# Moving LayerNorm steps, two stores and a vector sum around the down products of a fused attention and feed-forward kernel

## The chip, the cores and the metric

The kernel runs on one core of a Trainium2 chip. The metric is the time of one execution on the device in microseconds (us). Times given as start times count from the start of the profiled span. The engines are TensorE (PE in the profile, its weight load PEld), VectorE (DVE), ScalarE (ACT), GpSimd (POOL) and SyncE (SP). SyncE does no arithmetic here: it issues nearly all DMAs, in the order in which the program gives them.

## The reference

The input x has 2048 rows of 640 columns. It is normalised row by row; the normalised rows go into an attention with 32 heads of 192 columns over the last 512 keys of a cache, and into a gated feed-forward of width 1536. The two results are multiplied and added to x.

```python
x = A_x
xn = _layernorm(x, axis=-1)                  # (x - m) / sqrt(v + 1e-5)
q = (xn @ wq).reshape(B, Sq, 32, 192)        # 32 heads
k, v = the last W = 512 rows of k_cache, v_cache
p = softmax(q k^T * 192 ** -0.5)
s = (p v, heads side by side) @ wo
g = silu((silu(xn @ w_gate) * (xn @ w_up)) @ w_down)
return x + s * g
```

All inputs and the output are bfloat16.

## The kernel before

The kernel first does the feed-forward for all 2048 rows and leaves g in DRAM (`g_d`); then come the attention and the output product. The order of the work is written out by hand: each engine runs its instructions in the order in which the program emits them, and an engine that has to wait holds up all that is queued behind it on the same engine.

**Blocks and tiles.** The rows are cut into four blocks of 512 rows, numbered 0 to 3, and each block into four tiles of 128 rows, tile t = 4 * block + ti. `normalise(b, ti)` does two things to a tile: `ln_apply` subtracts the mean and scales the rows, in place in `rows_x` (on ScalarE for block 2, L411; on VectorE for blocks 1 and 3, L421), and `ln_transpose_dma` has SyncE issue a DMA transpose that puts the tile into `xnT` (L427), where columns are on partitions. The statistics of block 3 are gathered on ScalarE by eight small steps (`ln_sums`, L391 for sums, L395 for squares); they stand in the list `act_work`, and each call of `act_step()` emits the next of them.

**Halves and pairs.** Blocks 0 and 1 are half 0, blocks 2 and 3 half 1. The hidden layer of a half is computed in 2 x 2 form over the two blocks and over pairs of weight column groups, with seven products W1 to W7 in place of eight (a Strassen-Winograd scheme). `paired(half, g, n)` returns the steps `w1` to `w7` of one pair, each with ten matmuls (L695), and the copies, gates and sums between them. The products need sums of the two blocks: `swap_block` copies a block with its upper and lower partition halves exchanged (two DMAs, L646), which gives `x2s` and `x3s` of a half; `x_sum(half, n, part)` makes X1 to X4 from them on VectorE in two parts each (L655, shown in the profile at the line L490 of the helper `total`). For half 1, X1 is block 3 minus block 2, X2 is x3s minus X1, X3 is x3s minus block 3, and X4 is x2s minus X2. W2 of a pair uses x2s, W5 uses X1, W6 X2, W7 X3, W3 x3s. X1 of half 1 is written over the `rows_x` rows of block 3, so it needs these rows transposed first, as it needs `xnT` of both blocks.

**Downs.** `ffn_down(b, u)` does the down product of two tiles of block b, u = 0 or 1, again as seven products W1 to W7, each of six matmuls (L518). Its steps are numbered n = 0 to 6, in the order w1, w2, w6, w5, w7, w3, w4. ScalarE copies partial results and applies the outer SiLU (`gate`, L524) into the two tiles `g[0]` and `g[1]`, out of a pool of four `g_t` buffers. The last two gates of a down are kept back in the list `trailing`, and then two stores in the list `stores`; `finish_down` emits both, or with `False` the gates alone. A store (L527) is a DMA to `g_d`.

**The order around the change.** `run_pairs(0, ...)` ends with the last pair of half 0. Then the four downs of half 0 run in the order (b, u) = (1, 0), (1, 1), (0, 0), (0, 1), numbered m = 0 to 3; between their steps the loop of L1016 places the remaining statistics, the normalisation of blocks 2 and 3, the swaps x2s and x3s of half 1, and `load_pairs(0)`, eight DMAs with the weights of the second column group (L318 and L319). After the loop come `x_sum(1, 0, ...)`, further loads, and the pairs of half 1. After the pairs of half 1, `q_full` computes the first six q tiles in full (five matmuls each, L748, and a copy on ScalarE, L752), the first two directly one after the other and the others among the downs of half 1. PSUM tiles of two banks come from `sc_tile()` (two buffers, `sc`) and `mm_tile()` (`mm`).

Of the kernel before, what the change touches and what calls it, by code (L numbers as in the profile page):

```python
# [15 lines left out]
def kernel(  # L16
# [13 lines left out]
    nc = tc.nc  # L30
# [47 lines left out]
    def sc_tile():  # L78
        return sc_pool.tile([P, 2, 512], f32, name="sc")
# [172 lines left out]
    def q_of(i, j):  # L252
        pr, b = divmod(i, NB)
        half, k = divmod(b, 2)
        return q_pair(phase_of(pr, half))[:, 2 * k + j, :] if j < 2 else q_joint(half)[:, 2 * k + pr % 2, :]
# [4 lines left out]
    with ExitStack() as fctx:  # L260
# [243 lines left out]
        def ffn_down(b, u, then=None):  # L504
# [19 lines left out]
                nc.scalar.activation(g[side][:, n * HC : (n + 1) * HC], x, ACT.Silu)  # L524

            def store(side):
                nc.sync.dma_start(out=g_d[4 * b + u + 2 * side, :, :], in_=g[side][:])  # L527

            early_half = b == 2 and u == 0

# [72 lines left out]
        def finish_down(send=True):  # L603
            while trailing:
                trailing.pop(0)()
            while send and stores:
                stores.pop(0)()
# [133 lines left out]

            return dict(w1=w1, keep=keep, w2=w2, w5=w5, w6=w6, w7=w7, w3=w3, w4=w4, gate_2=gate_2, gate_3=gate_3, gated=gated)

        def q_full(i, j):
            pr, b = divmod(i, NB)
            q_ps = sc_tile()[:, 0, :]
            for c in range(NC):
                nc.tensor.matmul(  # L748
                    q_ps[:, :], w_all[:, weights_of(pr, j)[0], weights_of(pr, j)[1], c, :], xnT[:, c, b * 512 : (b + 1) * 512],
                    start=(c == 0), stop=(c == NC - 1),  # L750
                )
            nc.scalar.copy(q_of(i, j), q_ps[:, :])  # L752

        def swap_x(to, half, b):

# [189 lines left out]
        def run_pairs(half, steps, work, extra, k0=0):  # L945

            b0 = (1, 2)[half]
            earlier = steps[k0 - 1] if k0 else None
            for k in range(k0, len(steps)):
                final = k == len(steps) - 1  # L950
                now = steps[k]
                if k == 2:
                    earlier["w7"]()
                now["w1"]()
                if k == 1:
                    earlier["w3"]()
                now["keep"]()
                act_step()
                if earlier:
                    if k != 2:  # L960
                        earlier["w7"]()
                    if not final:
                        earlier["gate_3"]()
                now["w2"]()
                for do in work.get(k, ()):
                    do()
                if final:
                    if half == 0:
                        left_sum(b0, 0, 2)
                        wd_sum(2)  # L970
                    now["w6"]()
                    earlier["gate_3"]()
                    now["w5"]()
                    earlier["w4"]()
                    earlier["gate_2"]()
                    earlier["gated"](3)
                    now["w7"]()
                    if half:
                        earlier["gated"](2)
                    now["gate_3"]()  # L980
                    now["w3"]()
                    now["gated"](3)
                    downs = ffn_down(b0, 0, (b0, 1))
                    downs.pop(0)()
                    now["w4"]()
                    if half == 0:
                        ahead_1.append(ffn_down(1, 1, (0, 0)))
                    now["gate_2"]()
                    if half == 0:
                        nc.scalar.copy(p1_1, owns[1][:, 1, 0:HC])  # L990
                        act_step()
                        for n in range(2):
                            left_sum(b0, 0, n)
                        gated_late.extend(step["gated"] for step in (earlier, now))
                    if half:
                        now["gated"](2)
                        for n in range(2):
                            left_sum(b0, 0, n)
                    return downs
                now["w5"]()  # L1000
                if earlier:
                    earlier["w4"]()
                    earlier["gate_2"]()
                    for which in (3, 2):
                        earlier["gated"](which)
                now["w6"]()
                if k:
                    now["w3"]()
                earlier = now
                if k in extra:  # L1010
                    extra[k]()
# [4 lines left out]
        for m, (b, u) in enumerate(order):  # L1016
            if m:
                downs = ahead_1[0] if m == 1 else ffn_down(b, u, order[m + 1] if m < 3 else None)
            for n, do in enumerate(downs, 7 - len(downs)):
                do()  # L1020
                if n == 0:
                    finish_down(m != 2)
                if (m, n) in ((0, 3), (1, 0)):
                    act_step()
                if (m, n) in ((1, 6), (2, 3)):
                    for ti in range(2 * m - 2, 2 * m):
                        normalise(3, ti)
                    if m == 2:
                        finish_down()
                        swap_block(x2s, 2)  # L1030
                if (m, n) in ((1, 3), (1, 5)):
                    normalise(2, (n + 1) // 2)
                if m == 2 and n == 4:
                    swap_block(x3s, 3)
                    load_pairs(0)
                if m == 0 and n == 2:
                    wd_sum(3)
                if m == 1 and n == 3:
                    for gated in gated_late:
                        gated(2)  # L1040
        finish_down()
        mm_next[0] = 0
        for b in (2, 3):
            hTs[b] = ffh.tile([P, NF, 512], bf, name="hT")
        for part in range(2):
            x_sum(1, 0, part)
        load_k(0)
        for half in range(2):
            swap_x(DIFF[0], half, half)
# [43 lines left out]
        beside_x(ROWS[1], DIAG)  # L1093
        xwork += sum_x(0) + sum_x(1) + combined_x(ROWS[0], DIFF[1]) + combined_x(ROWS[1], DIAG)
        order = [(b, u) for b in (2, 3) for u in range(2)]
        for _ in range(2):
            q_full(*early_q.pop(0))
        for m, (b, u) in enumerate(order):
            if m:
                downs = ffn_down(b, u, order[m + 1] if m < 3 else None)  # L1100
            for n, do in enumerate(downs, 7 - len(downs)):
                do()
                if n == 0:
                    finish_down()
                if (m, n) == (3, 6):
                    finish_down()
                if (m, n) == (0, 1) or n == 6 and m:
                    q_full(*early_q.pop(0))
                if (m, n) == (2, 4):
                    copy_wq(1, (2,), nc.scalar.copy)  # L1110
                if (m, n) == (0, 4):
                    copy_wq(0, (2,), nc.scalar.copy)
                    load_wq(1)
                for _ in range(((5,), (2, 4, 6), (2, 4, 6), (3,))[m].count(n)):
                    xwork.pop(0)()
# [758 lines left out]
```

## Time and profile before

| | us |
|---|---|
| median of 3 runs | 856.94 |
| range of the runs | 856.87 to 856.99 |
| the profiled execution, whole | 856.42 |
| the profiled execution, span from first to last instruction | 854.6 |
| PE busy | 847.7 |
| VectorE busy | 640.9 |
| ScalarE busy | 472.2 |

The page of the profile gives the busy time of each engine, the DMA queues and the chain of work that ended last. The waits name who waited for whom, and the timeline gives instructions in order of start, neighbours of one kind merged: start, duration, engine, line, operation, output and inputs, count, and in brackets the idle time ahead of it and what ended it. Consecutive matmuls overlap, so that their durations do not add up; the distance between starts is what one costs. SPq and ACTq are the DMA issues in the queues of SyncE and ScalarE.

### The profile page before, as it was taken

How to read it: one execution, taken by the hardware profiler on the slowest of the kernel's cores; microseconds unless marked ns; L12 is line 12 of the kernel's file. 1: busy time of each engine (PE TensorE's matmuls, PEld its weight loads, DVE VectorE, ACT ScalarE, POOL GpSimd, SP SyncE). 2: the span in 40 equal slices, each digit the busy share in tenths (PEclk: the TensorE clock that was granted, in tenths of full speed). 3: DMA queues.
4: the chain of work that ended last, by engine and by line, in shares of the span. 5: the costliest groups of instructions: out<-in, count | busy, mean ns of one | idle time of the engine just before them, and what ended most of it. 6: DMA issues, size and time to landing. Idle time of an engine off the chain costs nothing.

```text
span 854.6 us, 24104 instructions
## 1 busy us (share of the span) xinstructions
PE 847.7 (99%) x10180; PEld 582.7 (68%) x10185; DVE 640.9 (75%) x1113; ACT 472.2 (55%) x638; POOL 173.2 (20%) x259
## 2 busy tenths in 40 slices
PE   9999999999999999999999999999999999999998
PEld 5656556576667667666667667667667777877877
DVE  6797997777758757767767757757757698978787
ACT  5785675657666676676676667667676500001010
POOL 1100000103423323323423323333322000000001
PEclk9999999999999999999999999999999999999999
DMA  9916927646797799998999998899687998191820
GB/s 238 256 16 142 218 76 170 133 94 159 174 172 139 195 180 183 196 208 187 203 192 198 196 173 150 165 213 200 158 178 164 292 273 325 23 329 55 311 82 28
DMA packets 272236, 150.51 MB, mean 176 GB/s; under 512 B 174208, under 2 KB 268032, under 8 KB 272128
## 3 DMA queue, kind: packets, MB, share of 16 engines
q1 hardware_dynamic: 271344, 148.33, 77.6%
q8 instruction: 80, 1.31, 0.6%
q10 hardware_dynamic: 784, 0.65, 0.3%
q14 instruction: 28, 0.23, 0.1%
HBM read 78.54 MB, written 30.41 MB: 127 GB/s over the span
## 4 chain that ended last, share of the span: by engine, by line
PE 97%; DMA 2%; DVE 0%; ACT 0%; issue 0%; SPq 0%; DVEq 0%; ACTq 0%
PE sc L1213 20%; PE acc L1367 16%; PE mm L1251 13%; PE mm L1156 13%; PE sc L1156 7%; PE sc L1251 6%; PE mm L695 4%; PE acc L1563 4%; PE sc L695 3%; PE mm L518 3%; PE sc L436 2%; PE sc L518 2%; PE mm L1144 1%; PE sc L748 1%; DMA xc<-xnT 1%; DMA fa<-in_B_w_gate_dram 1%
## 5 line engine op out<-in xcount | busy, mean ns | idle before, releaser
L1217 ACT ACTIVATE p_t<-sc 128x1024 bf16<-128x1024 f32 x256 | 256.9, 1025 | 93.7 <-PE sc L1213 93.0
L1213 PE MATMUL sc<-q_all,khat 64*128 64x512 bf16 x1536 | 204.2, 376 | 0.0
L1251 PEld LDWEIGHTS <-p_t 64*128 64x128 bf16 x4096 | 179.9, 94 | 35.7 <-POOL turn_t L1229 0.7
L1251 PE MATMUL mm<-V_p,p_t 64*128 64x193 bf16 x2784 | 146.7, 243 | 0.0
L1156 PEld LDWEIGHTS <-w_all 64*128 64x128 f16 (+1 forms) x1540 | 86.7, 94 | 73.3
L1156 PE MATMUL mm<-xc,w_all 64*128 64x512 f16 x950 | 119.3, 376 | 0.0
L1213 PEld LDWEIGHTS <-khat 64*128 64x128 bf16 x1536 | 82.6, 94 | 51.2 <-issue 2.2
L1198 POOL TENSOR_TENSOR m_f<-m_f 128x1024 f32<-128x1024 f32 x44 | 104.8, 2382 | 41.4 <-DVE q_all L1194 40.1
L1194 DVE TENSOR_TENSOR q_all<-mm,m_f 128x1024 bf16<-128x1024 f32 x44 | 53.8, 1223 | 68.9 <-ACT m_f L1191 68.9
L1367 PEld LDWEIGHTS <-a_q 128*128 128x128 bf16 (+1 forms) x888 | 84.0, 98 | 29.5
L1367 PE MATMUL acc<-b_w,a_q 128*128 128x320 bf16 (+2 forms) x720 | 95.7, 295 | 0.0
L1229 POOL MEMSET turn_t<- 128x1 f32 x128 | 12.8, 100 | 317.6 <-PE mm L1251 225.1
L1273 DVE TENSOR_TENSOR O_b<-mm,r 128x384 bf16<-128x384 f32 x142 | 73.8, 553 | 3.2 <-DVE r L1269 0.2
L1204 DVE TENSOR_TENSOR q_all<-mm,m_f 128x1024 bf16<-128x1024 f32 x44 | 53.8, 1222 | 22.9 <-POOL m_f L1198 22.5
L1251 PE MATMUL sc<-V_p,p_t 64*128 64x193 bf16 x1312 | 68.0, 243 | 0.0
L1191 ACT COPY m_f<-sc 128x1024 f32<-128x1024 f32 x37 | 37.5, 1012 | 29.1 <-PE sc L1156 28.9
L1156 PE MATMUL sc<-xnT,w_all 64*128 64x512 bf16 x370 | 46.5, 376 | 0.0
L1507 DVE TENSOR_TENSOR a_q<-a_q 128x3072 f16<-128x3072 bf16 (+1 forms) x24 | 41.8, 1754 | 5.7 <-PE acc L1367 4.2
L695 PEld LDWEIGHTS <-f_more 64*128 64x128 f16 (+1 forms) x480 | 26.3, 94 | 27.4 <-issue 3.9
L1269 DVE RECIPROCAL r<-mm 128x4 f32<-128x4 f32 x87 | 15.7, 180 | 35.5 <-PE mm L1251 33.7
L173 DVE TENSOR_TENSOR w_all<-wq_rows 64x640 f16<-64x640 bf16 x90 | 38.7, 482 | 1.0 <-DMA wq_rows<-in_A_wq_dram 0.5
L1388 POOL TENSOR_TENSOR xc<-xc,xg 128x320 f32<-128x320 f32 x2 | 1.8, 916 | 172.4 <-DVE xc L1404 172.4
(213 smaller groups left out, 1079.7 us busy)
## 6 DMA issues: line engine op xcount, KB each, us to landing
o_d<-OT_b SPq DMA_DIRECT2D x64, 384.0 KB, 3.8
a_q<-o_d SPq DMA_DIRECT2D x32, 768.0 KB, 6.1
wq_rows<-in_A_wq_dram SPq DMA_DIRECT2D x16, 480.0 KB, 5.6
b_w<-in_A_wo_dram SPq DMA_DIRECT2D x16, 480.0 KB, 6.2
wq_rows<-in_A_wq_dram SPq DMA_DIRECT2D x30, 240.0 KB, 6.5
K_p<-in_A_k_cache_dram SPq DMA_DIRECT2D x32, 192.0 KB, 3.5
V_p<-in_A_v_cache_dram SPq DMA_DIRECT2D x32, 192.0 KB, 4.1
xc<-xnT SPq DMA_DIRECT2D x14, 320.0 KB, 5.7
```

The lines of the kernel that those rows point to most:

```text
L518: nc.tensor.matmul(ps, left[:, c, :], D_OF[m][:, c, :], start=(first and c == 0), stop=(c == KD - 1), skip_group_check=True,)
L695: nc.tensor.matmul(ps[:, h, :], left[m][r, c, n * P : (n + 1) * P], right[m][r, c, :], start=(first and c == 0), stop=(c == NC - 1), skip_ ...
L1156: nc.tensor.matmul(ps[:, h, :], ws[h][r, c, :], xs[h][r, c, :], start=(first and c == 0), stop=(c == NC - 1), skip_group_check=True,)
L1194: nc.vector.tensor_tensor(to[:, 1:3, :], st["ps"][:, :, :], m_f[:, 5:3:-1, :], ALU.add)
L1198: nc.gpsimd.tensor_tensor(SIDE, diag, SIDE, ALU.subtract)
L1204: nc.vector.tensor_tensor(to[:, 0:4:3, :], st["ps"][:, :, :], SIDE, ALU.add)
L1213: nc.tensor.matmul(sc[:, h, :], khat[r, j, ks], q_of(i, j)[r, :], start=(j == 0), stop=(j == 2))
L1217: nc.scalar.activation(p_t[:, :, :], sc[:, :, :], ACT.Exp, scale=scale)
L1251: m = nc.tensor.matmul(acc[:, k, h * 256 : h * 256 + Dh + 1], Ps[i][kc][r, h, qt * P : (qt + 1) * P], V_of[i // NB % 2][r, kc, h, 0 : Dh + 1],
L1273: nc.vector.tensor_tensor(O_b[:, k, :, :], a_k[:, :, 0:Dh], r[:, k, :, :].to_broadcast([P, 2, Dh]), ALU.mult,)
L1367: nc.tensor.matmul(ps[:, 0:w], at[:, c, :], b_w[m][:, c, k * w : (k + 1) * w], start=(first and c == 0), stop=(c == KH - 1), skip_group_ch ...
L1507: nc.vector.tensor_tensor(a_s[n, m], x, y, op)
```

## The change

- The two stores of down (1, 1) are issued by ScalarE and no longer by SyncE, and they stand ahead of the last two normalisations of block 3 in the program.
- One `act_step` is emitted in the last pair of `run_pairs`, behind `gate_2` of the pair before, and no longer at step 3 of down m = 0.
- Tiles 2 and 3 of block 2 are normalised at step 3 of downs m = 0 and m = 1, and no longer at steps 3 and 5 of m = 1.
- The swap x3s of half 1 is emitted directly behind x2s, and `load_pairs(0)` at step 0 of m = 3, behind the stores of down (0, 0); before, both stood at step 4 of m = 2.
- The two parts of X1 of half 1 are computed at steps 3 and 5 of m = 3, and no longer after the loop.
- The first two q tiles share one PSUM tile, one in each of its banks: ten matmuls, then two copies.

```diff
             def store(side):
-                nc.sync.dma_start(out=g_d[4 * b + u + 2 * side, :, :], in_=g[side][:])
+                (nc.scalar if (b, u) == (1, 1) else nc.sync).dma_start(out=g_d[4 * b + u + 2 * side, :, :], in_=g[side][:])
...
-        def q_full(i, j):
+        def q_full(*units):
+            ps = sc_tile()
+            for n, unit in enumerate(units):
+                q_matmuls(*unit, ps[:, n, :])
+            for n, unit in enumerate(units):
+                nc.scalar.copy(q_of(*unit), ps[:, n, :])
+
+        def q_matmuls(i, j, q_ps):
             pr, b = divmod(i, NB)
-            q_ps = sc_tile()[:, 0, :]
             for c in range(NC):
...
-            nc.scalar.copy(q_of(i, j), q_ps[:, :])
...
                     earlier["gate_2"]()
+                    act_step()
                     earlier["gated"](3)
...
                 if n == 0:
                     finish_down(m != 2)
-                if (m, n) in ((0, 3), (1, 0)):
+                    if m == 3:
+                        load_pairs(0)
+                if m == 2 and n == 3:
+                    finish_down()
+                if (m, n) == (1, 0):
                     act_step()
                 if (m, n) in ((1, 6), (2, 3)):
                     for ti in range(2 * m - 2, 2 * m):
                         normalise(3, ti)
                     if m == 2:
-                        finish_down()
                         swap_block(x2s, 2)
-                if (m, n) in ((1, 3), (1, 5)):
-                    normalise(2, (n + 1) // 2)
-                if m == 2 and n == 4:
-                    swap_block(x3s, 3)
-                    load_pairs(0)
+                        swap_block(x3s, 3)
+                if n == 3 and m < 2:
+                    normalise(2, 2 + m)
+                if m == 3 and n in (3, 5):
+                    x_sum(1, 0, (n - 3) // 2)
...
-        for part in range(2):
-            x_sum(1, 0, part)
...
-        for _ in range(2):
-            q_full(*early_q.pop(0))
+        q_full(*(early_q.pop(0) for _ in range(2)))
...
-                    q_full(*early_q.pop(0))
+                    q_full(early_q.pop(0))
```

## The prediction

> **What bounds the kernel now.** I read the page first, for the engine that sets the end.
>
> ```profile
> span 854.6 us, 24104 instructions
> PE 847.7 (99%) x10180; PEld 582.7 (68%) x10185; DVE 640.9 (75%) x1113; ACT 472.2 (55%) x638; POOL 173.2 (20%) x259
> PE 97%; DMA 2%; DVE 0%; ACT 0%; issue 0%; SPq 0%; DVEq 0%; ACTq 0%
> ```
>
> TensorE (PE) carries 97% of the chain that ended last. An edit that adds no matmul and removes none can move the time only by the small holes in PE's row. Second view: the waits of PE over the whole span. Besides two waits while the kernel starts up, and one for instruction issue of which I speak below, it has these three.
>
> ```profile
> PE sc L695 <- DMA xc<-xnT: 0.4, 1, 0.4
> PE sc L518 <- ACT q_all L571: 0.3, 1, 0.3
> PE sc L695 <- DVE hT L490: 0.3, 1, 0.3
> ```
>
> Matmul ends are modelled, so the true size of a hole is read from starts. Third view: PE's timeline where the downs of half 0 end and the pairs of half 1 begin.
>
> ```profile
> 78.33 0.98 PE L518 MATMUL mm<-wd_sb,khat 128*128 128x320 f16 x6
> 79.62 0.97 PE L518 MATMUL sc<-wd_sb,q_all 128*128 128x320 bf16 x6 [0.31 <-ACT q_all L571]
> 80.43 0.98 PE L518 MATMUL mm<-w_all,hT 128*128 128x320 f16 x6
> 81.34 1.25 PE L695 MATMUL mm<-xnT,f_more 64*128 64x512 bf16 x10
> 83.17 1.24 PE L695 MATMUL sc<-xc,f_more 64*128 64x512 bf16 x9 [0.37 <-DMA xc<-xnT]
> 84.05 1.44 PE L695 MATMUL mm<-xnT,f_more 64*128 64x512 bf16 x10
> 87.29 1.57 PE L695 MATMUL mm<-rows_x,f_more 64*128 64x512 f16 x10
> 89.17 1.26 PE L695 MATMUL sc<-rows_x,f_more 64*128 64x512 f16 x10 [0.31 <-DVE hT L490]
> ```
>
> A down product of six matmuls takes 0.81 us (79.62 to 80.43), a pair product of ten 1.08 (three of them lie between 84.05 and 87.29: 3.24). Hole 1: 78.33 to 79.62 is 1.29, so 0.48 too long. Hole 2: 81.34 to 84.05 holds two pair products, 2.71 against 2.16: 0.55. Hole 3: 87.29 to 89.17 is 1.88 against 1.08: 0.80. Together 1.83 us, and that is the ceiling of what this change can give here.
>
> Fourth view, the chain in order of time through the same stretch, tells what each hole waited for.
>
> ```profile
> 76.69 2.00 DMA g_d<-g_t
> ...
> 80.34 5.96 DMA xc<-xnT
> ...
> 87.98 1.15 DVE hT L490
> ```
>
> ```profile
> 74.23 0.47 ACT L524 ACTIVATE g_t<-q_all 128x320 bf16<-128x320 f32 x1 [0.98 <-DVE q_all L490]
> ...
> 78.78 0.47 ACT L524 ACTIVATE g_t<-q_all 128x320 bf16<-128x320 f32 x1 [0.59 <-DMA g_d<-g_t]
> ```
>
> Hole 1: ScalarE's timeline, the second fence, has a gate of down (0,1) at 78.78 that sat 0.59 for a store of down (1,1), issued at 76.69 and landed at 78.69, because its g tile is one of four buffers; ScalarE then reaches the copy of w5 late, and W3 waits for that copy. Hole 2 is W2 waiting for x2s, the swapped block 2. Hole 3: the second half of x3s, the swapped block 3, issued at 80.34, lands at 86.30; VectorE makes X2 from it, then drains the second pair's V bank (until 89.13), and W5 needs that bank. From landing to PE's start: 89.17 - 86.30 = 2.87. All three holes are late work of SP's queue, so the fifth view is its timeline.
>
> ```profile
> 68.39 1.21 SPq L427 DMA_TRANSPOSE xnT<-rows_x  x1
> 71.13 2.55 SPq L427 DMA_TRANSPOSE xnT<-rows_x  x2
> 73.77 1.51 SPq L427 DMA_TRANSPOSE xnT<-rows_x  x1
> 75.37 1.23 SPq L427 DMA_TRANSPOSE xnT<-rows_x  x1
> 76.69 1.00 SPq L527 DMA_DIRECT2D g_d<-g_t  x2
> 77.80 4.00 SPq L646 DMA_DIRECT2D xc<-xnT  x4
> ```
>
> The transposes go out back to back: tile 2 of block 2 at 68.39, tile 3 behind it, block 3's four from 71.13, the last at 75.37; then the two stores of down (1,1), then the four halves of x2s and x3s.
>
> **Part 1: stores and LayerNorm moves (SP's queue).** The stores leave SP, so x2s follows the last transpose without the 77.80 - 76.69 = 1.11 us that they took. The LayerNorm applications of tiles 2 and 3 of block 2 come one place earlier each, at (0,3) and (1,3); the second takes the place of the first, so tile 3's transpose can go at 68.39, and SP is free when block 3's rows are.
>
> ```profile
> 70.33 0.80 DVE L421 TENSOR_SCALAR rows_x<-rows_x,mv,rstd 128x640 bf16<-128x640 bf16 x2
> 79.60 0.49 DVE L490 TENSOR_TENSOR q_all<-mm,q_all 128x320 f32<-128x320 f32 x1 [1.67 <-ACT q_all L571]
> 81.04 1.55 DVE L490 TENSOR_TENSOR rows_x<-xnT 128x1024 f16<-128x1024 bf16 x2
> 84.50 1.23 DVE L490 TENSOR_TENSOR hT<-sc,q_all 128x1024 bf16<-128x1024 f32 x1 [1.91 <-ACT q_all L705]
> ```
>
> Block 3's first application is half of the 0.80 at 70.33 and does not move; its rows are ready by about 70.8. So the transpose that went at 71.13 goes at 70.8, 0.33 earlier, and everything behind it on SP too. Sum for x2s: 0.33 + 1.11 = 1.44 us earlier, at 76.36. x3s follows at once as before (its position moves from n = 4 to n = 3, but nothing stood between on SP). The weight loads of the pairs (load_pairs(0)) now stand behind the stores of down (0,0) instead of ahead of them; both come after x3s and cannot delay it.
>
> Hole 1: ScalarE issues the stores behind the copy of w5 of down (0,0), in the idle time that starts at 73.25 (74.23 - 0.98); at the 2.00 of the chain they land before 76, and the gate needs them at 78.78 - 0.59 = 78.19. Since the gate comes 0.59 earlier and the hole is 0.48, the hole goes whole. Hole 2: x2s was complete at 83.17; 1.44 earlier is 81.73. W2's turn without hole 1 is 81.34 - 0.48 + 1.08 = 81.94, so hole 2 goes as well, with 0.2 to spare. Hole 3: x3s lands at 86.30 - 1.44 = 84.86; by then VectorE has drained the first V bank (84.50 + 1.23 = 85.73, less the 1.03 of the first two holes: 84.70), so it is not later than the landing, and W5 starts at 84.86 + 2.87 = 87.73. Without any hole its turn is 89.17 - 1.83 = 87.34. So 0.39 us of hole 3 stays, and the gain is 89.17 - 87.73 = 1.44 us.
>
> **Part 2: what ScalarE takes on.**
>
> ```profile
> 1.96 0.45 ACTq L291 DMA_DIRECT2D fa<-in_B_w_up_dram  x1
> ...
> 57.05 1.06 ACT L726 ACTIVATE q_all<-q_all 128x1024 bf16<-128x1024 f32 x1 [0.82 <-DVE q_all L490]
> ...
> 62.55 0.83 ACT L395 ACTIVATE f_more<-rows_x,mv 128x640 bf16<-128x640 bf16 x1
> 63.28 0.19 ACT L395 ACTIVATION_READ_ACCUMULATOR f_more<-rows_x,mv 128x1 f32 x1
> ```
>
> A DMA issue costs ScalarE about 0.45. Two are 0.90 and go into the 0.98 idle ahead of 74.23; if they took 0.2 more, that gate alone would wait, and nothing on PE reads it. The sum of squares that moves up between gate_2 and gate_3 of the last pair costs 63.47 - 62.55 = 0.92 and meets 0.82 idle: at most 0.1 late for gate_3, whose product is needed three vector steps on by W6 of down (1,0). Cost between 0 and 0.1; I take 0, since the idle nearly covers it. An application takes the place that this step leaves at (0,3): like for like.
>
> **Part 3: X1 (x_sum(1, 0)) among the downs.** The two parts, 1.55 at 81.04, move to after w5 and after w3 of down (0,1). VectorE was idle 1.67 ahead of 79.60. The first part now waits for block 3's last transpose; behind it stands the sum of w5, which must free U before W4.
>
> ```profile
> xnT<-rows_x SPq DMA_TRANSPOSE x1, 2.6
> ```
>
> That transpose, issued at 75.37, lands 2.6 later, at 77.97, and now 0.33 sooner: 77.64, ahead of VectorE, which is free at 79.60 - 1.67 = 77.93. The first part is two chunks of five, 0.62 of the 1.55, and the sum of w5 is due at 79.60 - 0.48 = 79.12; so W4 slips only if the landing passes 78.5. I take 0, with 0 to 0.3. Taking 1.55 away at 81.04 brings nothing by itself there, since VectorE next waits for W2 at 84.50.
>
> **Part 4: two q tiles in one PSUM tile.**
>
> ```profile
> 129.38 2.10 PE L748 MATMUL sc<-xnT,w_all 128*128 128x512 bf16 x9 [0.16 <-issue]
> ```
>
> Nine of ten matmuls are recorded, so the 0.16 is the missing first one; PE does not wait for a bank here. The same matmuls in the same order, the copies in the same order: 0, with at most the 0.16 either way.
>
> **Sum.** 1.44 off the profiled execution (856.42 in all, span 854.6): 854.98. That execution is 0.52 below the median of the three runs, 856.94; the same 1.44 off the median is 855.50.
>
> **The rivals.** Measurement can tell about 0.2%, that is 1.71 us. My 1.44 stays within it.
>
> *The ceiling.* The issue at 73.77 took 1.51 where its neighbours took 1.23. If that was a passing disturbance, x2s comes 0.28 earlier still, x3s gains 1.72, and with a little more from a less loaded DMA path all 1.83: 855.1, faster by over 0.2%. For: the other issues of the six run evenly. Against: nothing in the trace says that the 1.51 was chance.
>
> *The DMA engines, not SP.*
>
> ```profile
> 74.00:76.00 2.00, 2.00 (x17) 1.45 (x15) 1.97 (x5) 0.47 (x1) 0.00 (x0) 1.00 1.11 122
> ```
>
> In the stretch 74 to 76 the engines are fully taken by transposes (DMA share 1.11, the last column but one). The stores, moved there from 76.69, add their bytes; if the queue of packets pushes the last transposes and x2s back by as much as SP saved, 1.11, only 0.33 of gain is left: 856.6. The Trainium skill, page "DMA: Bandwidth & Descriptors", section "Issuing engines are not separate DMA queues", says that DMAs of all issuing engines run on the same 16 engines and that a second issuer saves only issue time; by that rule the stores' bytes are still paid, and the sum would be the 856.6 of this rival. Against it: only the last two transposes lie behind the stores, and x2s is gated by their issue, not their landing.
>
> *Slower: the store on ScalarE's queue lands late.*
>
> ```profile
> DMA to landing us min/median/max: 1.8/1.9/8.1
> ```
>
> These stores have taken up to 8.1 us to land when loads stood ahead of them. Issued at 73.3 and 73.8 beside the transposes, the second would land at 81.9, its gate run at 82.0 and, 0.84 later as before (78.78 to 79.62), W3 start at 82.8. From a W3 without a hole (78.33 + 0.81 = 79.14) to W5's hole-free turn at 87.34 are 8.20, so W5 would come at 91.0, 1.83 later than now: 858.8, slower by a little over 0.2%. The gain is gone from a landing at 80.05 on, 6.3 us after issue. Against: the transposes' share leaves gaps, and at 76.69 the same stores took 2.0.
>
> *Given back.* VectorE's first weight sum of the second group needs gate weights.
>
> ```profile
> 86.57 0.62 SPq L318 DMA_DIRECT2D fa<-in_B_w_gate_dram  x1
> fa<-in_B_w_gate_dram SPq DMA_DIRECT2D x1, 240.0 KB, 7.3
> 95.03 1.15 DVE L623 TENSOR_TENSOR fa<-fa 128x1920 f16<-128x1920 bf16 x1
> ```
>
> They land at 93.87, 1.16 before use. The use comes 1.44 earlier, at 93.59, and the loads 1.44 less the 1.00 of the two stores now ahead of them: 93.43, or, if they gain nothing, 93.87. VectorE may so wait up to 0.28; if PE had no slack behind it, the gain would shrink to 1.16: 855.8.
>
> **How the numbers follow.** Forecast 0.50 (855.5); ceiling 0.24; DMA engines 0.13; given back 0.05; slower 0.08. Faster by over 0.2% is the ceiling, 0.24; slower is its rival, 0.08; the rest, 0.68, is within. The range reaches from just below the ceiling's 855.1, with 0.2 for the spread between executions, to the 856.6 of the DMA rival: 854.9 to 856.6.
>
> **What would show it.** In the profile after: the first swapped half of x2s issued near 76.4 on SP directly behind the last transpose; no wait of a gate for a g_d store; W2 of the first pair starting 1.08 behind W1; the third hole still there at about 0.4, ended by VectorE; the early q products unchanged; the rest of the span shifted evenly. I am wrong if x2s is not issued earlier, if a hole of the same size opens elsewhere between 55 and 130, or if the third hole vanishes.

## The result and the profile after

The changed kernel took 855.79 us (median of 22 runs, 854.64 to 856.93) and the kernel before, on the same chip, 857.03 (22 runs, 856.32 to 857.81). The ratio is 0.9984 with a 95% interval of 0.9978 to 0.9991: a gain of 1.24 us or 0.16%, shown, but within the 0.2% that the prediction called no change. The profiled execution took 855.37 (span 853.6) against 856.42 (span 854.6).

The page of the changed kernel, its span, busy times and chain:

```profile
span 853.6 us, 24101 instructions
PE 847.4 (99%) x10180; PEld 582.5 (68%) x10185; DVE 641.0 (75%) x1113; ACT 471.6 (55%) x638; POOL 172.8 (20%) x259
PE 97%; DMA 1%; DVE 1%; ACT 0%; issue 0%; DVEq 0%
```

The busy times are those of before within 0.6. So the gain is to be looked for in the holes of PE's row. The waits of PE over the whole span, the two that lie in the stretch of the change:

```profile
PE sc L695 <- DMA xc<-xnT: 0.4, 1, 0.4
PE sc L695 <- DVE hT L490: 0.3, 1, 0.3
```

The wait for `q_all` (hole 1) is gone, the other two are still there. Their true size is read from starts, in PE's timeline of the changed kernel:

```profile
78.23 0.98 PE L518 MATMUL mm<-wd_sb,khat 128*128 128x320 f16 x6
79.05 0.98 PE L518 MATMUL sc<-wd_sb,q_all 128*128 128x320 bf16 x6
79.86 0.98 PE L518 MATMUL mm<-w_all,hT 128*128 128x320 f16 x6
80.77 1.25 PE L695 MATMUL mm<-xnT,f_more 64*128 64x512 bf16 x10
82.64 1.24 PE L695 MATMUL sc<-xc,f_more 64*128 64x512 bf16 x9 [0.41 <-DMA xc<-xnT]
83.53 1.44 PE L695 MATMUL mm<-xnT,f_more 64*128 64x512 bf16 x10
86.76 1.44 PE L695 MATMUL mm<-rows_x,f_more 64*128 64x512 f16 x10
88.52 1.26 PE L695 MATMUL sc<-rows_x,f_more 64*128 64x512 f16 x10 [0.31 <-DVE hT L490]
```

W7 to W3 is now 0.82, so hole 1 (0.48) is closed. Hole 2 is 83.53 - 80.77 - 2.16 = 0.60 (it was 0.55), hole 3 is 88.52 - 86.76 - 1.08 = 0.68 (it was 0.80). From W7 to W5 there are 10.29 us against 89.17 - 78.33 = 10.84 before: 0.55 gained where 1.44 was forecast. The rest of the gain lies almost 600 us later, where attention ends and the output product begins. PE's timeline there, of the kernel before, and then of the changed kernel:

```profile
674.06 1.51 PE L1251 MATMUL mm<-V_p,p_t 64*128 64x193 bf16 x32
675.90 3.42 PE L1367 MATMUL acc<-b_w,q_all 128*128 128x320 f16 x24 [0.33 <-ACT O_last L1279]
```

```profile
673.42 1.51 PE L1257 MATMUL mm<-V_p,p_t 64*128 64x193 bf16 x32
674.86 3.43 PE L1373 MATMUL acc<-b_w,q_all 128*128 128x320 f16 x24
```

Before, the first output product started 1.84 behind the last group of attention matmuls and waited for ScalarE's drain of `O_last`; now it starts 1.44 behind and waits for nothing: 0.40 gained, from an edit that the prediction priced at 0. The wait stood in the same view of the kernel before from which the prediction took its three holes (the waits of PE over the whole span):

```profile
PE acc L1367 <- ACT O_last L1279: 0.3, 1, 0.3
```

So the account of the profiled execution is 0.55 at the holes, 0.40 at the output product and 0.10 of an earlier start (W7 at 78.23, not 78.33), in all 1.05, as much as the two profiled times differ by.

Why the holes gave so little stands in SP's timeline of the changed kernel:

```profile
70.71 1.21 SPq L427 DMA_TRANSPOSE xnT<-rows_x  x1
72.01 2.44 SPq L427 DMA_TRANSPOSE xnT<-rows_x  x1
74.54 1.23 SPq L427 DMA_TRANSPOSE xnT<-rows_x  x1
75.86 1.24 SPq L427 DMA_TRANSPOSE xnT<-rows_x  x1
77.27 4.00 SPq L646 DMA_DIRECT2D xc<-xnT  x4
```

Block 3's first transpose goes out at 70.71, as forecast (70.8), and x2s follows the last one directly. But one issue took 2.44, where the slowest of before took 1.51, and x2s went at 77.27, not 76.36. The two theories at this point: (A) ScalarE's own issuing of the two stores holds SP's up; (B) something else stretches that one issue, and the stores at most add to it. The DMA view of the changed kernel, 72.5 to 73.6, and that of before, 73.2 to 73.9, show a candidate for B:

```profile
q8 instruction: 1, 0.02, 6.9%
g_d<-g_t ACTq DMA_DIRECT2D x2, 160.0 KB, 3.2
```

```profile
q8 instruction: 1, 0.02, 8.0%
```

In each, a single packet of 0.02 MB passes on queue q8, the queue of instructions. It takes 0.069 x 16 x 1.1 = 1.2 us of one DMA engine in the changed kernel, from 72.74 on, inside the issue of 2.44. In the kernel before it takes 0.080 x 16 x 0.7 = 0.9, from 73.31 on, and so reaches into the issue of 1.51 that began at 73.77.

### The profile page after: what moved, and what is told of

Read it like the earlier page. It is cut to its first block, busy times and chain, and to the rows that moved or that the text cites. A ratio compares the mean times of both kernels' runs of the same rounds, so it can differ in the third digit from the quotient of the medians.

```text
span 853.6 us, 24101 instructions
## 1 busy us (share of the span) xinstructions
PE 847.4 (99%) x10180; PEld 582.5 (68%) x10185; DVE 641.0 (75%) x1113; ACT 471.6 (55%) x638; POOL 172.8 (20%) x259
## 4 chain that ended last, share of the span: by engine, by line
PE 97%; DMA 1%; DVE 1%; ACT 0%; issue 0%; DVEq 0%
PE sc L1219 20%; PE acc L1373 16%; PE mm L1257 14%; PE mm L1162 13%; PE sc L1162 7%; PE sc L1257 6%; PE mm L695 4%; PE acc L1569 4%; PE mm L518 3%; PE sc L695 3%; PE sc L518 2%; PE sc L436 2%; PE mm L1150 1%; PE sc L754 1%; DMA xc<-xnT 1%; PE gu L436 0%
## 5 line engine op out<-in xcount | busy, mean ns | idle before, releaser
L1279 DVE TENSOR_TENSOR O_b<-mm,r 128x384 bf16<-128x384 f32 x142 | 73.9, 553 | 3.2 <-DVE r L1275 0.2
```

The source lines that it names most:

```text
L1279: nc.vector.tensor_tensor(O_b[:, k, :, :], a_k[:, :, 0:Dh], r[:, k, :, :].to_broadcast([P, 2, Dh]), ALU.mult,)
```

## The experiments

Spans and starts of single executions differ by about 1 us (W7 of down (0,1) starts between 78.21 and 79.30 in the kernels below), largely since PE waits a varying time, up to 1.3, for the first weights at the start of the kernel. So the whole kernels are compared by ratio and interval, and a single mechanism by distances within one trace. Each ratio is to the kernel before, run on the same chip.

### The q pair, alone and taken out

```diff
# pair_only: the kernel before with this alone; no_pair: the changed kernel without it
-        for _ in range(2):
-            q_full(*early_q.pop(0))
+        q_full(*(early_q.pop(0) for _ in range(2)))
```

> The kernel before with one part of the change alone: the first two q tiles share one PSUM tile. Theory: the pair takes one sc tile less, so every later sc tile of the kernel stands in the other of the two buffers, and the first output product (acc) no longer falls on the banks that ScalarE drains last. The wait of PE for O_last on ScalarE (0.33 in the profile before, at 675.90) is gone, worth about 0.38 us; the three holes between 78 and 90 stay at 0.48, 0.55 and 0.80. Time 0.4 us below the kernel before. Rival: the 0.38 in the profile after was chance or came from an earlier start of PE; then the wait is there again and the time is that of before within 0.1.

> The changed kernel with the first two q tiles in a PSUM tile each, as before. Theory (parity of the sc buffers): the wait for O_last comes back with 0.3, the stretch from 78 to 90 stays as in the changed kernel; 0.4 us above the changed kernel, 0.6 to 0.9 below the kernel before. Rival (chance): no wait for O_last, time as the changed kernel, 1.0 to 1.2 below before.

The pair alone: 856.59, ratio 0.9993 (0.9985 to 1.0002). The changed kernel without it: 855.41, ratio 0.9985 (0.9976 to 0.9994). PE's timeline at the first output product, first of the pair alone, then of the changed kernel without it:

```profile
674.62 1.51 PE L1255 MATMUL mm<-V_p,p_t 64*128 64x193 bf16 x32
676.07 1.12 PE L1371 MATMUL acc<-b_w,q_all 128*128 128x320 f16 x7
```

```profile
675.77 2.47 PE L1374 MATMUL acc<-b_w,q_all 128*128 128x320 f16 x17 [0.33 <-ACT O_last L1286]
```

The pair takes the wait away in the kernel before (distance 1.45), and without the pair the wait of 0.33 is back. The 0.40 belongs to part 4. It is too small for the intervals to show; the traces show it. In all nine traces with the pair the wait is gone; in the four of before, the stores alone, without the pair, and the unused tile of the next section it stands.

### Pairing or the turn of the buffers

Pairing takes one `sc` tile less. `sc` has two buffers used in turn, so all later tiles change places. To tell this from the pairing itself, one more tile is taken in the kernel before, once without and once with an instruction that writes to it (one column set to zero, a value that nothing reads).

```diff
         for _ in range(2):
             q_full(*early_q.pop(0))
+        sc_tile()                                      # parity_before
+        nc.vector.memset(sc_tile()[:, 0, 0:1], 0.0)    # parity_used
```

> The kernel before with one unused sc tile taken after the first two q tiles; no instruction is added, only the two buffers change places from there on. Theory (parity): PE's wait for O_last at the first output product is gone as with the pair, 0.38 less from 676 on, about 856.6 beside 857.0. Rival (the pairing itself, two banks drained behind ten matmuls, does it): the wait stays at 0.3 and the time is that of before.

> The kernel before with one more sc tile taken after the first two q tiles, of which VectorE sets one column to zero, so that the tile is used (the unused one changed nothing). Theory (parity of the two buffers): PE's wait for O_last at the first output product is gone, 0.35 to 0.4 less from 676 on, less some 0.1 for the added instruction if PE waits for it. Rival (the pairing itself does it): the wait of 0.3 stays and the time is that of before.

With the unused tile: 856.89, ratio 1.0000 (0.9991 to 1.0010). With the used one: 856.79, ratio 1.0000 (0.9991 to 1.0009). PE's timeline, unused and then used:

```profile
675.91 2.33 PE L1368 MATMUL acc<-b_w,q_all 128*128 128x320 f16 x16 [0.33 <-ACT O_last L1280]
```

```profile
675.95 1.26 PE L1368 MATMUL acc<-b_w,q_all 128*128 128x320 f16 x8
```

An unused tile doesn't turn the buffers and leaves the wait. A used one, with no pairing at all, removes it: the first output product comes 0.17 behind the last attention matmul there, 0.57 with the unused tile. So it is the turn, and the rival falls. That the first bank of the output product is then not the one that ScalarE drains last is read from the code and from the name of the wait; the traces don't show which of the two buffers an instruction uses. The execution with the used tile began 0.25 later than that of before (W7 at 78.58) and lost 0.19 more at hole 1 (0.67), so its time shows nothing of it.

### What stretches the issue on SP

The stores alone, in the kernel before; and the stores of the changed kernel on GpSimd's queue, so that ScalarE issues no DMA.

```diff
# stores_only: the kernel before with
-                nc.sync.dma_start(out=g_d[...], in_=g[side][:])
+                (nc.scalar if (b, u) == (1, 1) else nc.sync).dma_start(out=g_d[...], in_=g[side][:])
# pool_stores: the changed kernel with
-                (nc.scalar if (b, u) == (1, 1) else nc.sync).dma_start(out=g_d[...], in_=g[side][:])
+                (nc.gpsimd if (b, u) == (1, 1) else nc.sync).dma_start(out=g_d[...], in_=g[side][:])
```

> The kernel before with one part alone: the two stores of down (1,1) on ScalarE's queue. Theory: hole 1 (0.48) goes whole; x2s is issued up to 1.1 earlier (76.7 in place of 77.8 on the clock of before), less what a stretched transpose issue takes, so holes 2 and 3 together shrink by 0.3 to 1.1; at PE's eighth pair product 0.8 to 1.5 less than before, O_last's wait stays. 0.8 to 1.3 below before. Rival (the stores beside the transposes cost what they save): hole 1 goes and holes 2 and 3 grow by as much; same as before.

> The changed kernel with the two stores of down (1,1) issued by GpSimd in place of ScalarE. In the profile after, SP's issue of block 3's second transpose took 2.4 us and ScalarE's second store 1.25, both ending at 74.4. Theory A (ScalarE's issues hold up SP's): without DMA issues on ScalarE that transpose issues in 1.2 to 1.5, x2s goes out near 76.2 in place of 77.27, the last hole shrinks by about 1, and the time is 0.8 to 1.1 us below the changed kernel. Theory B (a 16 KB instruction fetch on one DMA engine, at 72.74, holds up every issue behind it): the issue again takes about 2.4, x2s goes out at 77.2 to 77.4, and the time is that of the changed kernel within 0.2.

The stores alone: 855.97, ratio 0.9991 (0.9982 to 1.0000), and hole 1 was closed by them alone. From W7 to W5 they gained 0.42, less than the 0.8 to 1.5 expected: holes 2 and 3, at 0.64 and 0.76, together did not shrink. On GpSimd: 855.61, ratio 0.9979 (0.9970 to 0.9988). SP's timeline, the stretched issue of each, stores alone first:

```profile
72.33 2.15 SPq L427 DMA_TRANSPOSE xnT<-rows_x  x1
```

```profile
73.54 2.60 SPq L427 DMA_TRANSPOSE xnT<-rows_x  x1
```

With no DMA issued by ScalarE the issue is still stretched, to 2.60. Theory A falls; that the stores themselves add to the stretch is not excluded.

The changed kernel once more tells what varies between executions.

> The changed kernel once more, beside the next three on the same chip. Theory: 1.0 to 1.4 below before; hole 1 gone, and one transpose issue of SP between 70 and 76 that overlaps the 16 KB fetch takes 1.9 to 2.5, so x2s goes out 0.4 to 1.0 earlier than before and not 1.4. Rival: the 2.4 was a chance of one execution; then all issues take 1.5 or less and the stretch from 78 to 89 gains 1.4.

855.57, ratio 0.9986 (0.9977 to 0.9995). Its timelines of SP and of PE:

```profile
73.43 1.77 SPq L427 DMA_TRANSPOSE xnT<-rows_x  x1
```

```profile
78.34 0.98 PE L518 MATMUL mm<-wd_sb,khat 128*128 128x320 f16 x6
...
87.96 1.26 PE L695 MATMUL sc<-rows_x,f_more 64*128 64x512 f16 x10 [0.31 <-DVE hT L490]
```

The same program: another of the four transposes is hit, the stretch is 1.77 and not 2.44, and from W7 to W5 there are 9.62, 1.22 less than before; hole 2 is gone. Hole 3 is 0.59. So the gain at the holes was 0.55 in one execution and 1.22 in another.

The last kernel of this group has no store beside the transposes: the g tiles of down (1,1) lie in a free part of `fa`, nothing waits for them, and SP issues their stores behind x3s.

```diff
# fa_g: the changed kernel with
+        g_11 = [fa_flat[:, 4096 + side * D : 4096 + (side + 1) * D] for side in range(2)]
...
-                    g[side] = ffa.tile([P, D], bf, name="g_t", bufs=4)
+                    g[side] = g_11[side] if (b, u) == (1, 1) else ffa.tile(...)[:, :]
...
-                (nc.scalar if (b, u) == (1, 1) else nc.sync).dma_start(...)
+                nc.sync.dma_start(...)
...
-                if m == 2 and n == 3:
-                    finish_down()
...
                         swap_block(x3s, 3)
+                        finish_down()
```

> The changed kernel with the two g tiles of down (1,1) put into a free part of the weight tile fa, so that no later gate waits for their stores, and the stores issued by SP behind x3s; no DMA on ScalarE, no store beside the transposes. The fetch of 16 KB is still there. Theory A (fetch and stores together stretched the issue to 2.4): the stretched transpose issue is back near 1.5, x2s goes out near 76.4 (on the clock of before), hole 2 is gone, hole 3 is 0.4 or less; 0.7 to 1.0 below the changed kernel, 2 below before. Theory B (the fetch alone): one issue still takes 2.4, x2s near 77.3, time as the changed kernel within 0.3. Either way hole 1 stays away.

856.25, ratio 0.9993 (0.9984 to 1.0003). SP's timeline, then PE's and VectorE's:

```profile
74.28 1.62 SPq L427 DMA_TRANSPOSE xnT<-rows_x  x1
```

```profile
79.18 0.98 PE L518 MATMUL mm<-wd_sb,khat 128*128 128x320 f16 x6
...
88.53 1.26 PE L696 MATMUL sc<-rows_x,f_more 64*128 64x512 f16 x10 [0.16 <-DVE hT L490]
...
99.35 1.26 PE L696 MATMUL sc<-rows_x,f_more 64*128 64x512 f16 x10 [0.93 <-DVE hT L490]
```

```profile
96.40 1.16 DVE L623 TENSOR_TENSOR fa<-fa 128x1920 f16<-128x1920 bf16 x1 [1.92 <-DMA fa<-in_B_w_gate_dram]
```

W7 to W5 is 9.35, a gain of 1.49 where the prediction had 1.44: up to here it is theory A of this run. Ten microseconds later most of it is lost again: the gate weights now come behind four stores, VectorE waits 1.92 for them, and PE 0.93 for VectorE (1.11 by the distance of starts, 97.16 to 99.35). This is the rival called *given back*, larger than it was priced.

A table of the six now says where x2s's advance went. The advance is the start of the first swapped half, measured from W7 of down (0,1): 77.80 - 78.33 = -0.53 in the kernel before. The excess is what the stretched issue took over the 1.51 of before.

| kernel | x2s from W7 | advance | stretched issue | advance + excess | forecast on SP |
|---|---|---|---|---|---|
| changed | -0.96 | 0.43 | 2.44 | 1.36 | 1.44 |
| changed, once more | -1.60 | 1.07 | 1.77 | 1.33 | 1.44 |
| without the pair | -1.48 | 0.95 | 1.93 | 1.37 | 1.44 |
| stores on GpSimd | -0.83 | 0.30 | 2.60 | 1.39 | 1.44 |
| no stores beside (`fa_g`) | -1.86 | 1.33 | 1.62 | 1.44 | 1.44 |
| stores alone | -0.92 | 0.39 | 2.15 | 1.03 | 1.11 |

The advance and the excess add up to the forecast within 0.11 in all six. The queue did what the prediction said; one issue took the rest. A packet of instructions on q8 overlapped the stretched issue in all of them. The issue never took longer than the 1.22 of its neighbours and the time for which the packet lay inside it: that was 1.22 in the changed kernel, 0.69 once more, 1.00 without the pair, 1.54 with the stores on GpSimd, 0.88 in `fa_g` and 0.94 with the stores alone. Against the packet as the whole cause stands an earlier transpose of the kernel before: it was issued at 43.11, a packet lay inside for 0.73, and it took 1.21. That the packet causes the stretch was not tried by itself, since no kernel here is without it. Nor is the share of the stores settled: stretched issues are 1.77 to 2.60 with stores beside them, and 1.49 to 2.00 without (the kernel before, the pair alone, the two with one more tile, `fa_g`, and the next two).

### Stores behind the loads, with and without the LayerNorm move

To keep `fa_g`'s gain, the g tiles go into a spare part of `f_more` and all four stores behind the weight loads. The second kernel is the same with the LayerNorm steps and the step of the statistics at their old places.

```diff
# g_more: as fa_g, but
+        g_11 = [more[:, 7 * NC * FW + (side + 1) * D : 7 * NC * FW + (side + 2) * D] for side in range(2)]
...
                         swap_block(x3s, 3)
+                        load_pairs(0)          # and all four stores at step 0 of m = 3
# g_more_ln_old: g_more with
-                    act_step()                 # in the last pair of run_pairs
...
-                if (m, n) == (1, 0):
+                if (m, n) in ((0, 3), (1, 0)):
                     act_step()
...
+                if (m, n) in ((1, 3), (1, 5)):
+                    normalise(2, (n + 1) // 2)
-                if n == 3 and m < 2:
-                    normalise(2, 2 + m)
```

> The changed kernel with the g tiles of down (1,1) in a part of the weight tile f_more that nothing uses until the second group's sums; SP issues x2s, x3s, then load_pairs(0), and the stores of downs (1,1) and (0,0) behind these. No store stands beside the transposes and none ahead of the weight loads. Theory: as with the tiles in fa, hole 1 is gone, x2s goes out near 76.4 on the clock of before and the stretch to PE's eighth pair product gains 1.5; and since the loads are no longer behind four stores, VectorE's wait near 95 and PE's 1.1 at 99 do not come. With the pair's 0.38: 1.8 to 2.0 below before, 0.6 to 0.9 below the changed kernel. Rival (what is gained ahead of the pairs is always taken back at the second group's sums, since VectorE has no room there): 0.5 or less below the changed kernel, with a wait of PE for hT of 0.5 or more near 99.

> As g_more, with the LayerNorm applications of tiles 2 and 3 of block 2 and the step of the statistics at their old places. Theory: the transposes of block 3 start behind block 2's as before, 0.33 later than in g_more; x2s goes out near 76.7 and hole 3 keeps 0.3 to 0.7 of its 0.80; 0.3 above g_more. Rival (the earlier LayerNorm is what makes the gain): 1.0 or more above g_more. Or it makes nothing: same as g_more within 0.1.

With the move: 855.25, ratio 0.9978 (0.9970 to 0.9987). Without: 855.42, ratio 0.9986 (0.9977 to 0.9995). The intervals overlap with each other and with that of the changed kernel in the same runs (0.9986), so no best version is shown. SP's timeline with the move, then without:

```profile
73.39 2.00 SPq L427 DMA_TRANSPOSE xnT<-rows_x  x1
...
76.82 0.61 SPq L646 DMA_DIRECT2D xc<-xnT  x1
```

```profile
73.72 1.61 SPq L427 DMA_TRANSPOSE xnT<-rows_x  x1
...
76.82 0.61 SPq L646 DMA_DIRECT2D xc<-xnT  x1
```

The move lets the third transpose go 0.33 earlier, exactly the 0.33 of the prediction, and that issue ends at 75.39 against 75.33: it gained nothing. In these two executions the issue that met the packet ended 1.07 behind the packet's end, whenever it began. From W7 to W5 the gain was 0.95 with the move and 1.00 without, where 1.5 was expected with it. Of the three expectations for the kernel without it, these traces fit the one that the move makes nothing; the times, 0.17 apart, don't settle it. VectorE's weight sum, with the move, has lost its wait:

```profile
94.04 1.15 DVE L623 TENSOR_TENSOR fa<-fa 128x1920 f16<-128x1920 bf16 x1
```

In the changed kernel's two executions it waited, 0.19 in the first and 1.14 in the second. The second, VectorE's timeline and then PE's:

```profile
95.05 1.16 DVE L623 TENSOR_TENSOR fa<-fa 128x1920 f16<-128x1920 bf16 x1 [1.14 <-DMA fa<-in_B_w_gate_dram]
```

```profile
96.59 1.26 PE L695 MATMUL sc<-xc,f_more 64*128 64x512 bf16 x10
98.00 1.26 PE L695 MATMUL sc<-rows_x,f_more 64*128 64x512 f16 x10
```

The two products start 1.41 apart, 0.33 too long. So the execution with the larger gain at the holes gave a third of a microsecond back here, and the two end alike (spans 853.6 and 853.5).

### The swap ahead of the transposes

If x2s is what hole 2 waits for, it could go first: on SP ahead of block 3's transposes, and in `fa_g` on GpSimd's queue at the same place.

```diff
# x2s_first: the changed kernel with; x2s_pool: fa_g with nc.gpsimd as issuer
+                if (m, n) == (1, 6):
+                    swap_block(x2s, 2)
...
-                        swap_block(x2s, 2)
```

> The changed kernel with the swap x2s issued ahead of block 3's four transposes (at step 6 of m = 1). Theory (SP's order, a queue that runs without a pause from 68 to 82, sets holes 2 and 3): x2s lands near 76, hole 2 (0.60 in the profile after) is gone; x3s no longer stands behind x2s and lands 4 to 5 us after its issue near 78.8, by 84.0, so hole 3 (0.68) shrinks to 0.1 or less; 1.1 to 1.3 us below the changed kernel, some 2.2 below before. Rival (the DMA engines are the limit): the 640 KB of x2s stretch block 3's transposes by about what they take themselves, x3s lands at 85.5 or later, hole 2 goes and hole 3 grows by as much; time as the changed kernel within 0.3.

> As fa_g, and x2s is issued by GpSimd ahead of block 3's transposes, so that its bytes share the DMA engines with them from another queue and do not stand ahead of them in SP's. Theory (the DMA engines have a third of their time free between 71 and 78): x2s lands by 80, the transposes' issue stretches by 1 to 2 in all, block 3's last lands by 79, x3s lands by 84.4 and all three holes are gone: 1.3 below the changed kernel. Rival (as with x2s ahead in SP's own queue, where one transpose issue took 4.2 and VectorE then held W4 for 3.1): the last transpose lands after 80, VectorE waits for it with the first part of X1 and W4 slips by 1 to 3; slower than the changed kernel by that.

On SP: 860.52 (5 runs), ratio 1.0039 (1.0025 to 1.0053), slower by 0.4%, which neither its theory nor its rival had. On GpSimd: 857.08, ratio 1.0003 (0.9994 to 1.0012), with W4 1.50 late, as its rival had it. The first one's timelines of SP, VectorE and PE, in that order:

```profile
73.20 4.19 SPq L427 DMA_TRANSPOSE xnT<-rows_x  x1
```

```profile
82.85 0.69 DVE L490 TENSOR_TENSOR rows_x<-xnT 128x1024 f16<-128x1024 bf16 x1 [4.19 <-DMA xnT<-rows_x]
```

```profile
84.00 1.76 PE L518 MATMUL mm<-w_all,hT 128*128 128x320 f16 x6 [3.06 <-DVE q_all L490]
```

The transpose behind the swap took 4.19 to issue (a packet on q8 lay inside for 0.88 of it), the first part of X1 waited 4.19 for the last transpose, the sum of w5 stood behind it, and W4 waited 3.06. This is the price that the prediction put on part 3, a landing past 78.5, made real. In the GpSimd form the same chain was 3.63 at the issue, 2.56 on VectorE and 1.50 on PE. In both, hole 3 was 0: X2 was early enough there, but what it cost was more.

## Why the prediction was right, and where its steps failed

- **The sum was right, two of its terms were not.** The forecast was 1.44 off, all of it from the three holes; the medians differ by 1.24. The profiled execution gained 1.05: 0.55 at the holes, 0.40 that part 4 was to bring nothing of, and 0.10 of start. That the time came out near the forecast 855.5 was in part luck: two errors offset each other. In the second execution the holes gave 1.22, but 0.33 was lost again at 98.
- **Hole 1: right.** It went whole, in the changed kernel and with the stores alone. The two issues took 1.63 and not the 0.90 of the prediction, and the gate behind them was late: VectorE had made its input by 74.10, and the gate began at 74.41, just behind the second issue's end at 74.36. The profile's name for that wait, VectorE, is the wrong one. It cost nothing, as the prediction had said of such a delay: no PE instruction reads that gate, and the next gate (77.99) waited for nothing. VectorE's sum, then ScalarE's timeline, in the changed kernel:

```profile
73.61 0.49 DVE L490 TENSOR_TENSOR q_all<-mm,q_all 128x320 f32<-128x320 f32 x1 [0.78 <-PE mm L518]
```

```profile
72.73 1.63 ACTq L527 DMA_DIRECT2D g_d<-g_t  x2
74.41 0.47 ACT L524 ACTIVATE g_t<-q_all 128x320 bf16<-128x320 f32 x1 [1.26 <-DVE q_all L490]
...
77.99 0.47 ACT L524 ACTIVATE g_t<-q_all 128x320 bf16<-128x320 f32 x1
```

- **x2s 1.44 earlier: the failed step.** On SP's queue the 0.33 and the 1.11 were there. Mis-sized was the 1.51 issue, carried over as it was; it measured 1.61 to 2.60 in the kernels whose queue ran earlier and had x2s behind the transposes. Why it is stretched stays open. In the two kernels that differ in the LayerNorm and statistics steps alone, the 0.33 was lost whole in that issue. x2s came 0.43 and 1.07 earlier in the two executions of the changed kernel, and hole 2 stayed in the one and went in the other.
- **Hole 3: the chain was right.** The chain of the changed kernel has its last half of x3s:

```profile
79.82 5.86 DMA xc<-xnT
```

  It lands at 85.68, and W5 starts at 88.52, 2.84 later; forecast was 2.87. The hole was 0.68 and not 0.39 because the landing came at 85.68 and not at 84.86; of these 0.82 the remaining hole 2 took most, since it delayed W5's turn as well.
- **Part 2: right, though the issues cost more.** Nothing on PE waits for what ScalarE took on, though the two issues took 1.63 and 1.67 in the two executions and not 0.90.
- **Part 3: right, and closer than it read.** Block 3's last transpose, issued at 75.86, landed at 78.48 and not at 77.64, for the same stretched issue; that is the very limit of 78.5. X1's first part began at 78.56, and W4 followed W3 at 0.81. The swap moved ahead showed what lies beyond the limit. VectorE's timeline in the changed kernel, with the weight sum of *given back* below it:

```profile
78.56 0.69 DVE L490 TENSOR_TENSOR rows_x<-xnT 128x1024 f16<-128x1024 bf16 x1 [0.73 <-issue]
...
94.65 1.16 DVE L623 TENSOR_TENSOR fa<-fa 128x1920 f16<-128x1920 bf16 x1 [0.19 <-DMA fa<-in_B_w_gate_dram]
```

- **Part 4: the other failed step.** The prediction said that besides start-up and issue PE had three waits over the whole span; it left out a fourth, the 0.3 for `O_last`. The bounds of 0.16 either way were taken from the q products themselves, where nothing did change. The effect was some 546 us later (129.38 to 675.90 in the kernel before), through the order in which two PSUM buffers are used.
- **The rivals.** *The ceiling* rested on the 1.51 being a passing disturbance; such an issue was in every execution of the table, so it was not. *The DMA engines* came near in the first execution, where 0.43 of the advance was left and the rival had 0.33, but not in the second, with 1.07. Its rule, that DMAs of all issuers share the same engines (the Trainium skill, "DMA: Bandwidth & Descriptors", section "Issuing engines are not separate DMA queues"), is not contradicted by the stretched issues of 1.77 to 2.60 beside the stores, but 2.00 without a store speaks against the stores' bytes as the whole cause. The same section of the Trainium skill calls the issue time usually small against the transfer; here the issues, 1.2 to 2.6 each back to back, set when x2s could go. *Given back* was priced at 0.28 on VectorE; it was 0.19 and 1.14. The price took 1.00 for the two stores now ahead of the loads; they held SP's queue for 2.87 and 2.78. *Slower* did not come: in the changed kernel no gate waited for a store.
- **The signs named ahead.** x2s directly behind the last transpose: seen, but at 77.27 and not near 76.4. W2 1.08 behind W1: wholly only in the second execution; in the first, nine of W2's ten matmuls waited for x2s. No gate waiting for a store and the early q products unchanged: seen in both. The third hole, ended by VectorE: seen, at 0.68 and 0.59 and not at 0.4. No new hole up to 130: true of the first execution, not of the second (0.33 at 98). The rest shifted evenly: not so, because of the 0.40 at the output product.

## What to carry to other kernels

When a queue that issues back to back sets the time of a later transfer, check each issue for its own length, and treat one that is longer than its neighbours as a cost that can come again and grow, not as a fixed term. Go through every wait that the view of the whole span lists, also those far from the edit. When an edit changes how many tiles a rotating pool hands out, follow the rotation to the end of the kernel: which buffer the last tiles fall into can open or close a wait hundreds of microseconds later. A step that frees a queue by putting it behind something must be followed to the next loads on that queue, where the gain may be given back.

## What the runs showed of the hardware

- Where x2s stood behind block 3's four transposes, one of the four took 1.49 to 2.60 to issue in every trace, overlapped by a packet of instructions on q8, and the others 1.20 to 1.27; which of the four is hit, and by how much, differed between two executions of one program (2.44 and 1.77).
- Behind the two swapped halves of x2s the issue of a transpose took 4.19, and 3.63 with the halves on GpSimd's queue; each time a packet on q8 lay inside, for 0.88 and 1.12 of it. SP's issue time is not fixed.
- A PSUM tile that is taken and never used did not turn the buffers; one column written by VectorE was enough to do so.
